# First batch by query tiles with its channel mix among the weight loads, score pieces in pairs, and x by head pair

## The chip, the core and the metric

One core of a Trainium2 chip runs the whole program. The metric is device time in microseconds (us) of one execution. The kernel before takes 312.73 us (median of 3 runs, 312.42 to 312.89). Five engines work side by side, each in the order in which its own instructions were written: TensorE (PE, with its weight loads as PEld), VectorE (DVE), ScalarE (ACT), GpSimd (POOL) and SyncE (SP), which here issues all DMAs. They wait for each other by semaphores.

## The reference

Blockwise causal attention, followed by an RWKV channel mix with a shift by one token.

```
q, k, v: (8 batches, 8 heads, 576 tokens, 64)     block = 64
scores = q @ k.T / 8, kept where query block >= key block
attn = softmax(scores);   x = (attn @ v) as (batch, token, head * 64 = 512)
x_prev = x shifted by one token, zeros at a batch's start
xk = mu_k * x + (1 - mu_k) * x_prev;   xr = the same with mu_r
k = relu(xk @ w_k)                (512 -> 1024)
out = sigmoid(xr @ w_r) * ((k * k) @ w_v)
```

All inputs and outputs are float32.

## The kernel before

**Attention, by batch.** The 576 tokens of a batch are four tiles of 128 and a tail of 64. For each of 4 head pairs `add_qk` loads q and k (four DMAs of 128 KB), POOL casts them to bf16, PE transposes them (8 matmuls of 128 columns), DVE copies the result out of PSUM into `t_qkt`; a tail transposes the last 64 tokens of all heads. `add_score` computes the scores of a head pair in three pieces (512, 64 + 448 and 320 + 192 query columns), with keys as the stationary operand. The two heads of a pair lie on partitions 0 to 63 and 64 to 127, so their two matmuls run side by side. ACT takes the exponential of each piece (128 x 1024) into `t_e`; POOL sets masked blocks to zero. `add_last` does the last 64 x 64 blocks of all heads. `add_av` multiplies by v (15 matmuls of 65 columns a head; the 65th column is the sum of the exponentials), and DVE normalises into x (`t_x`). When all heads of the batch are done, `add_xt` transposes x by token tiles, and ACT copies it to `t_xt`.

**Channel mix, by chunk.** The 8 x 576 tokens are 9 chunks of 512. `add_mix` makes xk and xr: a difference of neighbours (two on DVE, two on POOL), a repair of the column at a batch's start on both engines, and 8 multiply-adds on DVE. `add_pk` is xk @ w_k in 8 groups of 4 matmuls of 512 columns, relu on ACT, square on DVE; `add_pr` is xr @ w_r with tanh on ACT (4 groups of 4); `add_pv` is the second product (4 groups of 8), and DVE combines and SP stores it.

**What sets the order.** All of these are tasks of a planner (`Plan`). Each has an engine, an estimated length, a rank, the tasks that it depends on, and buffers of rings that it takes (`RINGS`: 10 load buffers, 2 score buffers `s`, 2 of `m` for transposes and the product with v, 2 of `mm` for the channel mix; these three are PSUM). The planner runs a list schedule over these estimates and writes the instructions out in that order, so ranks and estimated lengths decide what stands behind what on each engine. Batch b has ranks around 13 b, and batch 0 stands 40 lower (`step`, L174); chunk c's matmuls begin at `step(c + 1, 6) + LAG` (L693). The loads of w_k are ranked after batch 0's, and those of w_r and w_v after batch 1's (L656 to L674).

Of the kernel before, what the change touches and what calls it, by code (L numbers as in the profile page):

```python
# [9 lines left out]
FP = mybir.dt.float32  # L10
# [3 lines left out]
ALU = mybir.AluOpType  # L14


class Plan:
# [24 lines left out]
    def order(self):  # L42
# [8 lines left out]
        while waiting:  # L51
            moved, nxt = False, []
            for e, q in todo.items():
# [3 lines left out]
                for n, t in enumerate(q):  # L57
# [46 lines left out]
def kernel(  # L104
# [12 lines left out]
    nc = tc.nc  # L117
# [16 lines left out]
             "x": 1, "r": 4, "xt": 2, "d": 1, "xk": 2, "xr": 2, "kr": 3,  # L134
# [25 lines left out]
    MUR = consts.tile([P, CCn], FP)  # L160

# [35 lines left out]
    def add_qk(b, pr, rank):  # L197
        nb = plan.buf("nb")
        tiles["nbbuf", b, pr] = nb
        for n, src in enumerate((q, k)):  # L200
# [8 lines left out]
            def fn(n=n, key=key):  # L209
# [6 lines left out]
                "POOL", 0.62, rank, fn,  # L216
                [t] + ([cast["qk", b, pr, 0]] if n else []),
                takes=[nb] if n == 0 else [],
                uses=[ld] + ([nb] if n else []))

    def add_tail(b, rank):
# [12 lines left out]
        cast["tb", b] = on("POOL", 0.62, rank, fn, [t], takes=[tb], uses=[tl])  # L234

    def add_v(b, rank, halves):
        bufs = [plan.buf("vl") for _ in range(5)]
        for half in range(halves):
            nh = H // halves
            hs = slice(half * nh, half * nh + nh)  # L240
            for sc in range(5):
                n = P if sc < 4 else D
                t = load(("vl", b, sc),
                         (lambda: new("vl", [P, H, D], FP)) if half == 0 else None,
                         lambda d, n=n, sc=sc, hs=hs: [(
                             d[0:n, hs], v[b, hs, sc * P:sc * P + n].rearrange(
                                 "h p d -> p h d"))],
                         rank[half], 0.0011 * n * nh,
                         takes=[bufs[sc]] if half == 0 else [],
                         uses=[] if half == 0 else [bufs[sc]])  # L250

                def fn(n=n, sc=sc, hs=hs):
                    nc.gpsimd.tensor_copy(VOs[b % 2][0:n, sc, hs, 0:D],
                                          tiles["vl", b, sc][0:n, hs])
                first = half == 0 and sc == 0
                cast["v", b, half, sc] = on(
                    "POOL", 0.12 + 0.001 * nh * D, rank[half], fn,
                    [t] + ([] if first else [cast["v", b, 0, 0]]),
                    takes=[vo_buf[b]] if first else [],
                    uses=[bufs[sc]] + ([] if first else [vo_buf[b]]))  # L260

    def add_w(name, n, rank):
        src = {"k": moe_w_k, "r": moe_w_r, "v": moe_w_v}[name]
        src = src.rearrange("(cc p) (n j) -> n cc p j", p=P, j=C)
        for i in range(n):
# [4 lines left out]
                     rank, 0.7, takes=[ld])  # L270

            def fn(i=i, cc=cc, half=half):
# [9 lines left out]
                "DVE" if name == "k" else "ACT", 0.4 if name == "k" else 0.56,  # L282
# [5 lines left out]
    def add_qkt(b, pr, rank):  # L288
# [27 lines left out]
        def ev():  # L316
# [4 lines left out]
            if pr < HP:  # L321
# [22 lines left out]
    def add_score(b, pr, i, rank):  # L344
        s = plan.buf("s")
        if i == 0:
            tiles["ebuf", b, pr] = plan.buf("e")
        ebuf, qbuf = tiles["ebuf", b, pr], tiles["qktbuf", b]

        def fn():  # L350
            if i == 0:
                tiles["e", b, pr] = new("e", [P, 2, 3, 512], F16)
            PS = tiles["ps", b, pr, i] = new("s", [P, 2, 512], FP)
            qkt = tiles["qkt", b]
            for (col, kc, q0, n) in PIECES[i]:
# [24 lines left out]

    def add_last(b, rank):
# [30 lines left out]
    def add_av(b, h, rank, halves):  # L412
# [3 lines left out]
        if h == 0:  # L416
            tiles["xbuf", b] = plan.buf("x")
# [313 lines left out]
```

## Time and profile before

| | |
|---|---|
| median of 3 runs | 312.73 us |
| the profiled execution | 312.19 us |
| its span, first to last instruction | 310.4 us |
| PE busy | 274.2 us, 88% of the span |
| DVE, ACT, POOL busy | 225.2, 186.0, 124.8 us |
| first matmul starts, last one ends | 4.9 us, 305.5 us |
| read from HBM, written | 33.56 MB, 9.44 MB |

A matmul's busy time includes the time that it spends in the pipeline beside the next one, so busy shares of PE say only that it had something in flight; its throughput is read from the starts of consecutive groups. The granted clock (PEclk) has two levels here, 1.00 (2.4 GHz) and 0.50 (1.2 GHz).

### The profile page before, as it was taken

Reading aid. Unit: us, or ns where it says so; the run is one execution under the profiler, and the core shown is the slowest. Engines: PE = TensorE matmul, PEld = TensorE weight load, DVE = VectorE, ACT = ScalarE, POOL = GpSimd, SP = SyncE. Lnnn points to the kernel's source line nnn. Section 1 sums busy time; section 2 is a strip of 40 time slices with the busy share of each in tenths; the row PEclk is TensorE's granted clock in tenths of the full one; section 3 lists DMA queues with packets and bytes.
Section 4 is the critical chain, followed back from the end, with each engine's and each line's share of the span. In section 5 each row is a group of like instructions: output and inputs, shape, how many; then the busy total and the mean of one; then the engine's idle time right before and its main releaser. Section 6 shows DMA issues by size and latency. Waiting matters only on the chain. (4 is left out here: it accounts for less than half of the span.)

```text
span 310.4 us, 6718 instructions
## 1 busy us (share of the span) xinstructions
PE 274.2 (88%) x2512; PEld 150.5 (48%) x2512; DVE 225.2 (73%) x407; ACT 186.0 (60%) x269; POOL 124.8 (40%) x279
## 2 busy tenths in 40 slices
PE   1883889899569979999999999989999999889993
PEld 0452545366345634564456545644555456334441
DVE  3265589464989599849796978697869677998541
ACT  1761559968447737785678567855795584252530
POOL 3660772467957682473276224610033004120000
PEclk9998759999899999999999999999999999999998
DMA  6989999999999988999963610012001200201102
GB/s 155 220 193 246 205 235 363 212 220 199 206 230 240 229 213 221 205 208 231 241 140 81 143 68 2 2 64 74 1 2 55 83 2 34 99 7 68 68 34 102
DMA packets 122769, 43.44 MB, mean 140 GB/s; under 512 B 115568, under 2 KB 115568, under 8 KB 122736
## 3 DMA queue, kind: packets, MB, share of 16 engines
q1 hardware_dynamic: 122736, 43.01, 58.0%
q8 instruction: 19, 0.31, 0.5%
q14 instruction: 14, 0.11, 0.1%
HBM read 33.56 MB, written 9.44 MB: 139 GB/s over the span
## 5 line engine op out<-in xcount | busy, mean ns | idle before, releaser
L368 ACT ACTIVATE t_e<-t_s 128x1024 f16<-128x1024 f32 x96 | 95.7, 1026 | 48.6 <-PE t_s L358 48.3
L573 PE MATMUL t_mm<-t_xk,WK 128*128 128x512 f16 x288 | 70.2, 383 | 4.1 <-DVE t_xk L549 2.2
L626 PE MATMUL t_mm<-WV,t_k 128*128 128x512 f16 x288 | 67.3, 379 | 5.1 <-DVE t_o L636 4.8
L590 DVE TENSOR_TENSOR t_k<-t_kr 128x512 f16<-128x512 f32 x72 | 53.5, 756 | 11.8 <-ACT t_kr L584 11.6
L584 ACT ACTIVATE t_kr<-t_mm 128x512 f32<-128x512 f32 x72 | 43.1, 599 | 27.0 <-PE t_mm L573 24.8
L212 POOL CAST t_nb<-t_ld 128x512 bf16<-128x512 f32 x64 | 43.0, 680 | 36.8 <-DMA t_ld<-in_q_dram 19.6
L376 POOL MEMSET t_e<- 64x128 f16 x128 | 23.6, 199 | 82.0 <-ACT t_e L368 77.8
L626 PEld LDWEIGHTS <-t_k 128*128 128x128 f16 x288 | 27.2, 98 | 36.2 <-issue 8.3
L426 PEld LDWEIGHTS <-t_e 128*128 128x128 f16 x896 | 34.7, 99 | 17.4 <-issue 5.8
L573 PEld LDWEIGHTS <-WK 128*128 128x128 f16 x288 | 25.7, 98 | 34.8 <-issue 10.3
L358 PE MATMUL t_s<-t_qkt 64*128 64x512 bf16 (+4 forms) x320 | 37.6, 313 | 5.4 <-ACT t_e L368 3.2
L426 PE MATMUL t_m<-VO,t_e 128*128 128x65 f16 x896 | 38.9, 196 | 3.8 <-DVE t_x L444 2.9
L636 DVE SCALAR_TENSOR_TENSOR t_o<-t_t,t_mm 128x512 f32<-128x512 f32 x36 | 24.6, 684 | 23.3 <-PE t_mm L626 16.8
L603 PE MATMUL t_mm<-WR,t_xr 128*128 128x512 f16 x144 | 36.2, 380 | 0.0
L613 ACT ACTIVATE t_t<-t_mm 128x512 f32<-128x512 f32 x36 | 21.5, 597 | 21.9 <-PE t_mm L603 21.8
L444 DVE TENSOR_TENSOR t_x<-t_m,t_r 128x320 f32<-128x320 f32 x64 | 31.5, 492 | 2.2
L492 ACT COPY t_xt<-t_m 128x512 f32<-128x512 f32 (+1 forms) x44 | 20.8, 521 | 17.6 <-PE t_m L482 17.6
L523 POOL TENSOR_TENSOR t_d<-t_xt 128x512 f32<-128x512 f32 x18 | 23.8, 1336 | 18.0 <-issue 9.8
L523 DVE TENSOR_TENSOR t_d<-t_xt 128x512 f32<-128x512 f32 x18 | 19.6, 1119 | 15.4 <-ACT t_xt L492 15.3
L549 DVE SCALAR_TENSOR_TENSOR t_xk<-t_d,MUK,t_xt 128x512 f16<-128x512 f32 x36 | 30.1, 874 | 0.3
L303 PE MATMUL t_m<-identb,t_nb 128*128 128x128 bf16 x256 | 23.4, 240 | 6.9 <-POOL t_nb L212 6.6
L322 DVE COPY t_qkt<-t_m 128x1024 bf16<-128x1024 bf16 x32 | 21.6, 677 | 9.9 <-PE t_m L303 9.6
(39 smaller groups left out, 218.9 us busy)
## 6 DMA issues: line engine op xcount, KB each, us to landing
out_dram<-t_o SPq DMA_DIRECT2D x36, 256.0 KB, 2.0
t_ld<-in_q_dram SPq DMA_DIRECT2D x64, 128.0 KB, 3.4
t_ld<-in_k_dram SPq DMA_DIRECT2D x64, 128.0 KB, 3.4
t_vl<-in_v_dram SPq DMA_DIRECT2D x28, 256.0 KB, 4.7
t_ld<-in_moe_w_k_dram SPq DMA_DIRECT2D x8, 256.0 KB, 5.6
t_ld<-in_moe_w_v_dram SPq DMA_DIRECT2D x8, 256.0 KB, 5.8
t_vl<-in_v_dram SPq DMA_DIRECT2D x15, 128.0 KB, 3.8
t_tl<-in_q_dram SPq DMA_DIRECT2D x8, 128.0 KB, 4.2
```

The source lines that it names most:

```text
L212: nc.gpsimd.tensor_copy(tiles["nb", b, pr][:, n], tiles[key][:, :].rearrange("p t h d -> p t (h d)"))
L358: nc.tensor.matmul(PS[:, h, col:col + n], qkt[rows, pr, 1, kc * P:kc * P + P], qkt[rows, pr, 0, q0:q0 + n], start=True, stop=True)
L368: nc.scalar.activation(tiles["e", b, pr][:, :, i, :], tiles["ps", b, pr, i], AF.Exp, scale=ISQ)
L426: nc.tensor.matmul(PA[:, mt * D1:(mt + 1) * D1], stationary(b, h, kc, mt), VOs[b % 2][:, kc, h, 0:D1], start=(kc == 0), stop=(kc == mt))
L444: nc.vector.tensor_tensor(tiles["x", b][:, :, h * D:(h + 1) * D], view[:, :, 0:D], Rc[:, :].unsqueeze(2).to_broadcast([P, 5, D]), ALU.mult)
L523: (nc.vector if eng == "DVE" else nc.gpsimd).tensor_tensor(tiles["d", c][:, cc], x[:, cc, 1:CH + 1], x[:, cc, 0:CH], ALU.subtract)
L549: nc.vector.scalar_tensor_tensor(tiles[name, c][:, cc], tiles["d", c][:, cc], (MUK, MUR)[n][:, cc:cc + 1], tiles["xt", c][:, cc, 1:CH + 1] ...
L573: nc.tensor.matmul(ps, WK[:, cc, jc * P:(jc + 1) * P], tiles["xk", c][:, cc], start=(cc == 0), stop=(cc == CCn - 1))
L584: nc.scalar.activation(tiles["kr", c, jc], tiles["pk", c, jc], AF.Relu)
L590: nc.vector.tensor_tensor(tiles["k2", c][:, jc], KR, KR, ALU.mult)
L603: nc.tensor.matmul(ps, tiles["xr", c][:, cc, jt * P:(jt + 1) * P], WR[:, cc], start=(cc == 0), stop=(cc == CCn - 1))
L626: nc.tensor.matmul(ps, tiles["k2", c][:, jc, jt * P:(jt + 1) * P], WV[:, jc], start=(jc == 0), stop=(jc == JCn - 1))
```

## The change

Six things change.

1. Batch 0 is loaded, transposed, scored and multiplied by query tiles of 128 tokens rather than by head pairs (`add_qk_tile`, `add_first`, `add_first_av`, `add_first_xt`), and chunk 0's channel mix is done per tile (`add_first_mix`, `add_first_pk` with 128-column matmuls), with the loads of all weights among its own.
2. Scores of later batches are planned two pieces at a time (`add_scores`).
3. x is kept by head pair (`x` ring 4), transposed as soon as a head pair is done, and mixed per head pair (`add_xt`, `add_mix`, `d` ring 3 of a quarter's size).
4. The repair at a batch's start is two small products on POOL behind the multiply-adds; it leaves DVE.
5. Ranks stand in a table, estimated lengths are raised (0.62 to 0.68, 0.73 to 0.82 and the like), chunk c's matmuls begin at `step(c) + 25`.
6. The planner may take two buffers of one ring for one task.

```diff
+RANK = {
+ 'loads': ['q0', 'wk0', 'v0', 'mu', 'wk7', 'wk1', 'wv2', 'wk2', 'wk3',
...
-             "x": 1, "r": 4, "xt": 2, "d": 1, "xk": 2, "xr": 2, "kr": 3,
+             "x": 4, "r": 4, "xt": 2, "d": 3, "xk": 2, "xr": 2, "kr": 3,
...
+    def add_scores(b, items, rank):
...
+        for it in items:
+            s = plan.buf("s")
+            bufs.append(s)
+            takes.append(s)
...
+        def fn():
             qkt = tiles["qkt", b]
-            for (col, kc, q0, n) in PIECES[i]:
-                for h in range(2):
-                    rows = slice(h * D, h * D + D)
+            for it in items:
+                PS = tiles["ps", b, it] = new("s", [P, 2, 512], FP)
...
+                for pr, col, kc, q0, n in mms:
+                    for h in range(2):
+                        rows = slice(h * D, h * D + D)
+                        nc.tensor.matmul(
+                            PS[:, h, col:col + n],
+                            qkt[rows, pr, 1, kc * P:kc * P + P],
+                            qkt[rows, pr, 0, q0:q0 + n], start=True, stop=True)
...
+    FIRST = {
+        0: [(0, 0, [0], P, [0, 1, 2, 3])],
+        1: [(0, 512, [0, 1], P, [0, 1]), (0, 1024, [0, 1], P, [2, 3])],
+        2: [(1, 384 * pr, [0, 1, 2], P, [pr]) for pr in range(4)],
+        3: [(2 + pr // 2, 768 * (pr % 2) + 384 * i, [2 * i, 2 * i + 1], 192,
+             [pr]) for pr in range(4) for i in range(2)],
+    }
...
+    def add_xt(b, pr, rank):
...
+            for i in range(4):
+                src = (tiles["x", b, pr][:, i] if pr < HP
+                       else tiles["x", b, i][:, 4])
...
+    def add_mix(c, cc, rank):
...
+                    def fix(n=n, at=at, name=name):
+                        nc.gpsimd.tensor_tensor(
+                            tiles[name, c][:, :, at:at + 1],
+                            tiles["xt", c][:, :, at + 1:at + 2],
+                            (MUK, MUR)[n][:, :].unsqueeze(2), ALU.mult)
...
+    def add_first_pk(mt, g, rank):
...
+            for j in range(4):
+                jc = 4 * g + j
+                for cc in range(CCn):
+                    nc.tensor.matmul(
+                        ps[:, j * P:(j + 1) * P],
+                        WK[:, cc, jc * P:(jc + 1) * P],
+                        tiles["xk", 0][:, cc, ts], start=(cc == 0),
+                        stop=(cc == CCn - 1))
...
+        for n in range(0, len(order), 2):
+            add_scores(b, order[n:n + 2], r + n)
...
-        first = step(c + 1, 6) + LAG
+    for c in range(1, NCH):
+        first = step(c, R["moe"])
```

The order on SP at the program's start, before (`t_ld` are load buffers of q, k and weights, `t_tl` the tails, `t_vl` v; x4 means four in a row):

```order
L185 DMA t_vl<-in_v_dram 64x4x64
L659 DMA MUK<-in_moe_mu_k_dram 128x4x1
L660 DMA MUR<-in_moe_mu_r_dram 128x4x1
L185 DMA t_ld<-in_moe_w_k_dram 128x512 x8
L185 DMA t_ld<-in_q_dram 128x4x64 x2
L185 DMA t_ld<-in_k_dram 128x4x64 x2
...
L185 DMA t_vl<-in_v_dram 128x8x64 x4
L185 DMA t_vl<-in_v_dram 64x8x64
L185 DMA t_ld<-in_moe_w_r_dram 128x512 x4
L185 DMA t_ld<-in_moe_w_v_dram 128x512 x8
```

And now, on SP, from the program's first DMA to the tails of batch 0:

```order
L218 DMA t_ld<-in_q_dram 128x8x64
L218 DMA t_ld<-in_k_dram 128x8x64
L218 DMA t_ld<-in_moe_w_k_dram 128x512
L218 DMA t_vl<-in_v_dram 128x8x64
...
L218 DMA t_ld<-in_moe_w_k_dram 128x512 x2
L218 DMA t_ld<-in_moe_w_v_dram 128x512
L218 DMA t_ld<-in_moe_w_k_dram 128x512 x5
...
L218 DMA t_ld<-in_moe_w_r_dram 128x512 x3
...
L218 DMA t_ld<-in_moe_w_v_dram 128x512 x6
L218 DMA t_tl<-in_q_dram 64x8x64
L218 DMA t_tl<-in_k_dram 64x8x64
```

All weights now stand ahead of batch 0's tail and of all of batch 1's loads; before, w_r and w_v came behind batch 1's.

The order on PE in front of chunk 1's first channel-mix matmul, before (with tile numbers; `t_mm_1564` is that matmul's output, `VO0` with `t_e` the product with v of batch 2):

```order
L426 MATMUL t_m_1506<-VO0_130,t_e_1367 128x65
...
L390 MATMUL t_s_1526<-t_qkt_1456 128x64
...
L303 MATMUL t_m_1542<-identb_120,t_nb_1385 128x128
...
L573 MATMUL t_mm_1564<-t_xk_1324,WK_134 128x512
```

And now, on PE, the same place:

```order
L592 MATMUL t_m_1525<-VO0_130,t_e_1371 128x65
...
L592 MATMUL t_m_1546<-VO0_130,t_e_1371 128x65
...
L348 MATMUL t_m_1576<-identb_120,t_nb_1543 128x128
...
L427 MATMUL t_s_1585<-t_qkt_1139 128x320
...
L427 MATMUL t_s_1590<-t_qkt_1139 128x512
...
L662 MATMUL t_m_1600<-identf_125,t_x_1524 128x128 x4
L800 MATMUL t_mm_1611<-t_xk_1185,WK_134 128x512
```

Now chunk 1's matmuls begin behind the second head of batch 2 (t_m_1546), whose product needs all of batch 2's v; before they began behind its fifth.

The order on PE in a later batch, before (`t_s` are score buffers):

```order
L358 LDWEIGHTS t_qkt_2626
L358 MATMUL t_s_3166<-t_qkt_2626 128x512
L573 LDWEIGHTS WK_134
L573 MATMUL t_mm_3173<-t_xk_2946,WK_134 128x512
...
L303 MATMUL t_m_3181<-identb_120,t_tb_2264 128x128
...
L358 MATMUL t_s_3188<-t_qkt_2626 128x64
...
L358 MATMUL t_s_3188<-t_qkt_2626 128x448
L303 LDWEIGHTS t_nb_2643
```

And now, on PE, the same kind of place:

```order
L427 LDWEIGHTS t_qkt_2576
L427 MATMUL t_s_2960<-t_qkt_2576 128x512
...
L427 MATMUL t_s_2964<-t_qkt_2576 128x64
...
L427 MATMUL t_s_2964<-t_qkt_2576 128x448
L800 LDWEIGHTS WK_134
L800 MATMUL t_mm_2971<-t_xk_2193,WK_134 128x512
```

Two score buffers are now filled in one visit, where a channel-mix group and four transposes stood between them. Over the whole program PE changes from other work to scores 82 times before and 59 times now.

## Rows read from the trace of the kernel before

**Rows 1.** Stretches: PE, PEld, DVE, ACT, POOL busy (count), PEclk, DMA share, GB/s

```profile
0.00:18.30 18.30, 10.58 (x107) 6.50 (x107) 6.10 (x17) 7.66 (x8) 10.28 (x31) 1.00 0.93 192
18.30:28.50 10.20, 5.24 (x103) 3.48 (x99) 5.68 (x16) 5.70 (x6) 3.02 (x12) 1.00 0.82 224
28.50:35.30 6.80, 5.39 (x27) 4.38 (x28) 2.85 (x10) 2.72 (x5) 2.51 (x4) 0.50 1.07 209
...
38.80:45.60 6.80, 5.66 (x38) 2.93 (x38) 6.18 (x8) 4.08 (x6) 5.29 (x13) 0.50 1.02 222
45.60:60.00 14.40, 13.49 (x126) 6.94 (x125) 11.09 (x22) 13.21 (x24) 4.44 (x9) 1.00 1.03 300
60.00:79.60 19.60, 18.22 (x219) 11.09 (x219) 11.54 (x21) 15.41 (x22) 13.92 (x31) 1.00 1.06 204
79.60:91.80 12.20, 7.14 (x99) 5.10 (x99) 10.29 (x20) 5.17 (x6) 9.69 (x23) 0.86 1.08 233
...
200.00:260.00 60.00, 58.38 (x561) 31.68 (x559) 47.28 (x88) 39.06 (x57) 11.23 (x36) 1.00 0.10 36
```

**Rows 2.** Timeline of PE, chunk 1's first matmuls: start, length in us

```profile
88.74 0.81 PE L573 MATMUL t_mm<-t_xk,WK 128*128 128x512 f16 x3
91.80 1.46 PE L573 MATMUL t_mm<-t_xk,WK 128*128 128x512 f16 x6 [2.25 <-DVE t_xk L549]
```

**Rows 3.** Waits from 60 to 92 us: total, times, longest

```profile
PE t_m L426 <- DVE t_x L444: 2.6, 1, 2.6
...
PE t_mm L573 <- DVE t_xk L549: 2.2, 1, 2.2
```

**Rows 4.** Timeline of PE in a stretch without waits, 184 to 190 us

```profile
184.50 0.61 PE L303 MATMUL t_m<-identb,t_nb 128*128 128x128 bf16 x8
185.05 0.39 PE L358 MATMUL t_s<-t_qkt 64*128 64x512 bf16 x2
185.37 1.04 PE L573 MATMUL t_mm<-t_xk,WK 128*128 128x512 f16 x4
186.24 0.39 PE L303 MATMUL t_m<-identb,t_tb 128*128 128x128 bf16 x4
...
188.63 0.60 PE L426 MATMUL t_m<-VO,t_e 128*128 128x65 f16 x14
189.06 0.19 PE L426 MATMUL t_m<-VO,EL 128*128 128x65 f16 x1
189.09 0.61 PE L303 MATMUL t_m<-identb,t_nb 128*128 128x128 bf16 x8
189.54 1.89 PE L573 MATMUL t_mm<-t_xk,WK 128*128 128x512 f16 x8
```

**Rows 5.** Timeline of PE, transposes of x at 201 us

```profile
201.69 1.04 PE L482 MATMUL t_m<-identf,t_x 128*128 128x128 f32 x8
202.56 1.03 PE L603 MATMUL t_mm<-WR,t_xr 128*128 128x512 f16 x4
```

**Rows 6.** Page, GB/s moved in each of 40 slices of 7.76 us

```profile
GB/s 155 220 193 246 205 235 363 212 220 199 206 230 240 229 213 221 205 208 231 241 140 81 143 68 2 2 64 74 1 2 55 83 2 34 99 7 68 68 34 102
```

**Rows 7.** Page, costly groups: busy us, mean ns of one, idle before

```profile
L368 ACT ACTIVATE t_e<-t_s 128x1024 f16<-128x1024 f32 x96 | 95.7, 1026 | 48.6 <-PE t_s L358 48.3
...
L584 ACT ACTIVATE t_kr<-t_mm 128x512 f32<-128x512 f32 x72 | 43.1, 599 | 27.0 <-PE t_mm L573 24.8
```

**Rows 8.** Groups by line: last blocks' exponential, multiply-adds, the small edge copy

```profile
L549 DVE SCALAR_TENSOR_TENSOR t_xk<-t_d,MUK,t_xt 128x512 f16<-128x512 f32 x36 | 30.1, 874 | 0.3
...
L399 ACT ACTIVATE EL<-t_s 64x512 f16<-64x512 f32 x8 | 4.7, 589 | 0.6 <-PE t_s L390 0.2
...
L508 DVE COPY t_xt<-t_xt 128x4 f32<-128x4 f32 x8 | 1.7, 210 | 0.0
```

**Rows 9.** Timeline of ACT, copies of x of two sizes

```profile
31.30 0.59 ACT L492 COPY t_xt<-t_m 128x512 f32<-128x512 f32 x1 [7.08 <-PE t_m L482]
...
34.89 0.37 ACT L492 COPY t_xt<-t_m 128x256 f32<-128x256 f32 x1 [0.35 <-PE t_m L482]
```

**Rows 10.** Waits over the whole span: total, times, longest

```profile
PE t_s L358 <- ACT t_e L368: 3.2, 5, 1.0
```

More of the change, by code (lines that the diff above doesn't have):

```diff
@@ L233, in fn @@
                 tiles["tb", b], tiles["tl", b][:, :].rearrange("p h d -> p (h d)"))
[L234 to L260, printed above, removed]
@@ L262, in add_w, with add_v, fn @@
-    def add_w(name, n, rank):
+        cast["tb", b] = on("POOL", 0.68, rank, fn, [t], takes=[tb], uses=[tl])
+    def add_v(b, ranks):
+        for sc in range(5):
+            n = P if sc < 4 else D
+            vl = plan.buf("vl")
+            t = load(("vl", b, sc), lambda: new("vl", [P, H, D], FP),
+                     lambda d, n=n, sc=sc: [(
+                         d[0:n], v[b, :, sc * P:sc * P + n].rearrange(
+                             "h p d -> p h d"))],
+                     ranks[sc], 0.0088 * n, takes=[vl])
+            def fn(n=n, sc=sc):
+                nc.gpsimd.tensor_copy(VOs[b % 2][0:n, sc, :, 0:D],
+                                      tiles["vl", b, sc][0:n])
+            cast["v", b, sc] = on(
+                "POOL", 0.68, ranks[sc], fn, [t],
+                takes=[] if sc else [vo_buf[b]],
+                uses=[vl] + ([vo_buf[b]] if sc else []))
@@ new lines, in fn, with add_edge, edge @@
+                    px[:, cc * P:(cc + 1) * P], tiles["x", 0, mt][:, cc],
+                    identf, is_transpose=True, start=(cc == 0),
+                    stop=(cc == CCn - 1))
+        t = on("PE", 0.46, rank, fn, [evac["x0", mt, g] for g in range(2)],
+               takes=[m], uses=[tiles["xbuf", 0, mt]])
+        n, off = (P, 0) if mt < 4 else (D, D)
+        to_xt(key, 0, mt * P, n, off, None, [t], rank, [m])
+    mixed = {}
+    def add_edge(c, rank):
+        def edge():
+            nc.vector.tensor_copy(xt_tile(c)[:, :, 0:1],
+                                  tiles["xt", c - 1][:, :, CH:CH + 1])
+        take = not xt_parts[c]
+        t = on("DVE", 0.21, rank, edge, list(xt_parts[c - 1]),
+               takes=[xtbuf[c]] if take else [],
+               uses=[xtbuf[c - 1]] + ([] if take else [xtbuf[c]]))
+        xt_parts[c].append(t)
+        for x in range(CCn):
+            xt_of[c].setdefault(x, []).append(t)
@@ L585, in relu @@
                                  AF.Relu)
-        t = on("ACT", 0.56, SOON, relu, [t], takes=[kr], uses=[m])
+        t = on("ACT", 0.6, SOON, relu, [t], takes=[kr], uses=[m])
         def sq():
@@ new lines, in mu1 @@
+        nc.vector.tensor_scalar_add(MUR1, MUR, -1.0)
+    R = RANK
+    at = {x: -99 + i for i, x in enumerate(R["loads"])}
+    for mt in range(4):
+        add_qk_tile(mt, at[f"q{mt}"])
+    add_tail(0, at["t"])
+    add_v(0, [at[f"v{sc}"] for sc in range(5)])
+    t = on("SP", 0.6, at["mu"], mus, [])
+    mu_ready.append(on("DVE", 0.3, at["mu"], mu1, [t]))
+    for name, n in (("k", 8), ("r", 4), ("v", 8)):
+        add_w(name, n, [at[f"w{name}{i}"] for i in range(n)], R["cast " + name])
+    for n, mt in enumerate((0, 1, 2, 3, HP)):
+        add_qkt(0, mt, R["qkt0"][n])
```

544 lines of the change are left out of this document (356 added, 188 removed), and 17 rows, old and new, of the table RANK.

## The prediction

> **What bounds the kernel now.** I read the stretches first [rows 1]. From 91.8 us on PE has something in flight nearly always (58.38 of 60 us between 200 and 260), no other engine does (DVE 47.28), and the DMA share is 0.10 there: the second part is bound by PE. The first part is not. Up to 18.3 us PE works 10.58 us, then 5.24 of 10.20, and from 79.6 to 91.8 only 7.14 of 12.20, while the DMA share is 0.82 to 1.08. The granted clock is 0.50 (1.2 GHz) from 28.5 to 35.3 and from 38.8 to 45.6, each time behind a stretch with idle time. The first part is bound by the arrival of data and by chains through PE, ACT and DVE that have too little work of PE beside them.
>
> A busy share does not say how much PE got done, so I price its work by the starts of neighbouring groups where nothing waits [rows 4, 5]. Eight transposes take 189.54 - 189.09 = 0.45 us, 0.056 each. Four matmuls of 512 columns take 186.24 - 185.37 = 0.87 us, 0.2165 each. Fifteen matmuls of 65 columns take 189.09 - 188.63 = 0.46 us, 0.030 each. Eight f32 transposes of x take 202.56 - 201.69 = 0.87 us, 0.109 each. A visit to the scores costs extra: eight transposes ahead of scores take 185.05 - 184.50 = 0.55 us, 0.10 more than ahead of a channel-mix group, and the two score matmuls of 512 columns, which run side by side, take 185.37 - 185.05 = 0.32 us where 512 columns take 0.2165. So going in and coming out cost 0.20 us together.
>
> With these prices the program before has 960 products with v (28.8 us), 288 transposes (16.1), 160 of x (17.4), 720 channel-mix matmuls (155.9), scores of 51,200 columns per head of a pair (100 x 0.2165 = 21.7) and 82 visits (16.4): 256.3 us of work. PE is at it from 4.9 to 305.5 us, so some 44 us are lost to waits and the slow clock. Most of that goes before chunk 1's channel mix gets going at 91.80 us [rows 2]: the work in front of it is 315 products (9.5), 136 transposes (7.6), 40 of x (4.4), 80 matmuls of chunk 0 (17.3), scores (8.2) and 24 visits (4.8), together 51.8 us, and 0.6 more for the three matmuls at 88.74. So 39 us are lost up to 91.8 us, and 9 to 10 in the 213.7 us after it.
>
> **Part by part: PE's work.** Pairs of pieces cut the visits from 82 to 59: 23 x 0.20 = 4.6 us less. Chunk 0's first product is now 128 matmuls of 128 columns with a weight load each instead of 32 of 512. The nearest row is the transposes, which have the same shape and also a weight load each: 128 x 0.056 = 7.2 against 32 x 0.2165 = 6.9 us, 0.3 more. Below that it can't go, since the columns are the same; 0.05 more for each would be 6 us, but nothing in the rows points there. Batch 0's scores have the same number of columns. New total: 256.3 - 4.6 + 0.3 = 252.0 us.
>
> A page of the Trainium skill speaks against those small matmuls: "TensorE: Matmul & The Clock Gate", section "Back-to-back issue gap", gives some 81 ns for each of a stream of weight load and matmul pairs of 128 columns. By it they would cost 10.4 us, and the kernel up to 3.2 us more than I forecast, if PE were the last to be ready there. The trace does not agree: pairs of just this shape go at 56 ns [rows 4], and I keep to that.
>
> **Part by part: where chunk 1 begins.** In the new order of PE there stand in front of chunk 1's first matmul 270 products (8.1), 128 transposes (7.2), 44 of x (4.8), 48 matmuls of 512 columns (10.4), the 128 small ones (7.2), scores of 16,640 columns (7.0) and 21 visits (4.2): 48.9 us. Behind it are 252.0 - 48.9 = 203.1 us, before 256.3 - 52.4 = 203.9. So what follows is 0.8 us shorter, and where the waits in it stay as they are, the span is T + (310.4 - 91.8) - 0.8 = T + 217.8 us, where T is the time at which chunk 1's matmuls begin. The whole prediction is this T.
>
> T is bounded by DMA. The first matmul of chunk 1 stands behind the second head of batch 2, which needs all of batch 2's v. Of q, k and v a batch has 3.54 MB, the weights 5.24 MB: 3 x 3.54 + 5.24, less the last head pair of batch 2 (0.52, loaded later), plus four stores of chunk 0 (1.05) is 16.4 MB. The slices of 7.76 us add up to 16.4 MB at about 72 us [rows 6]; their first ones hold idle time of the DMAs (shares of 0.93 and 0.82 [rows 1]) that the new order, which asks for all weights at once, can fill in part. So 67 to 72 us for the last byte, and 1.5 us for cast and products: T is not under 68.
>
> T is also bounded by ACT. Batch 0's tile 3 waits for the tail, now loaded behind all the weights and most of batch 0: 8.4 MB. At the slices' own rates that is 41 us; with weights at the 363 GB/s of the slice that held mostly weights and the rest at 205 it would be 5.24 / 0.363 + 3.15 / 0.205 = 30 us after a start of 2.5. So tile 3's exponentials begin between 34 and 43 us. From there ACT has, in its order up to the products of batch 2's first head pair, 15 exponentials of 1.026 (15.4), 8 of three quarters of that size (0.8 each by size, 6.4), three for the last blocks (1.8), four relu and two tanh of 0.6 (3.6) [rows 7, 8], and copies of x: two of 0.59, two of 0.37 [rows 9], and four pairs that I take at 0.75, since each splits 512 columns in two (4.9 in all): 32 us. ACT was busy 92% of the densest stretch and 79% of the one after it [rows 1]. From 34 us at full load T would be 67, from 43 us at 75% it would be 87. I take the middle, 38 us and 85%, with 1.5 us for the last zeros and products: T = 78. That is the step on which most depends.
>
> What else stands in this part. Chunk 0's 32 small multiply-adds on DVE (128 columns) replace eight of 512: between the edge copy's 0.21 us and half of 0.874 each [rows 8], 7 to 14 us in place of 7. DVE has by my count some 60 us of work up to T, so up to 15 us more can hide in its gaps; if it did not, T would stand at the upper end. The repair at a batch's start leaves DVE for POOL, which adds about 0.3 us ahead of a chunk whose mix is ready long before it is needed: nothing. The edge copy stays. More but smaller copies of x cost ACT 0.7 us a batch; it was idle a third of the time from 200 to 260 us, so nothing. The stores of chunk 0 stand on SP in front of batch 1's and 2's later loads and could hold them up while PE is late; that is in the 72 us.
>
> Mixing by head pair also removes what held PE between 79.6 and 91.8 us: 2.6 us for DVE to normalise while it was in a block of multiply-adds, and 2.2 us for the last of the mix [rows 3]. Next to be late there are ACT's exponentials, which the bound above holds.
>
> **Sum.** Span 78 + 217.8 = 295.8 us. The profiled execution took 312.19 us with a span of 310.4, so 1.8 more outside it: 297.6 us. Its time is 0.5 us under the median of the runs shown, so I predict 297.5 us.
>
> **Rivals.**
> 1. The early start does not come off: T stays near 91.8, since DMA and ACT give out the same work at the same rate, and only the visits are saved. 91.8 + 217.8 + 1.8 = 311.4 us. For it speaks that DMA was full from 28.5 us on; against it that chunk 0's 17 us of channel mix, which stood behind all of batch 0 and in the middle of batch 1, can now run while the weights land.
> 2. Pairs make PE wait. With two score buffers, a pair's second piece can't start before the exponential of the previous pair's second piece is done, and PE takes its work in order. There are 42 full pairs. If each costs PE half an exponential (0.51 us), that is 21.5 us: 297.6 + 21.5 = 319 us, slower. From (312.7 - 297.6) / 42 = 0.36 us a pair it is slower than before. Against it: before, PE waited for ACT ahead of scores 5 times in all, 3.2 us [rows 10], and ACT is busy 39 of 60 us in the part that would suffer.
> 3. It goes better: T at the DMA bound of 69 us, and the waits after it halve from 10 to 5 us, as the planner's lengths are now nearer to the measured ones. 69 + 217.8 - 5 + 1.8 = 284 us.
>
> **Chances and range.** The forecast (T from 68 to 88) 0.77, rival 1 0.10, rival 2 0.06, rival 3 0.07. T from 68 to 88 gives 287.6 to 307.6 us; half of rival 3 lies near that, and nearly all of rival 1 above it. I set 286 to 309 us. A measurement of this kernel tells 0.2% (0.6 us) from no change. Of rival 1 I count half as faster and half as the same: faster 0.77 + 0.07 + 0.05 = 0.89, same 0.05, slower 0.06.
>
> **What would show it.** Chunk 1's first channel-mix matmul starts near 78 us and nothing of 2 us or more holds it up behind that; chunk 0's small matmuls follow each other at 0.056 us at the full clock; a visit with two pieces costs 0.20 us above its columns, and there are 59; PE waits little for ACT ahead of scores. It is wrong if T is above 88, if the clock is at 0.50 for more than the 17 us that it was before 92 us, or if the stretch from T to the end takes more than 222 us, which would be rival 2.

## The result and the profile after

The changed kernel takes 302.0 us (median of 4 runs, 300.1 to 303.9); the kernel before took 312.6 us beside it. The ratio is 0.967, with an interval of 0.960 to 0.974. In a later series it took 303.5 us (6 runs, 300.2 to 304.2; ratio 0.970, 0.965 to 0.974). The forecast was 297.5 us, with a range of 286 to 309: the side and the range are right, the time is 4.5 us too low, 6.0 in the later series. Slow executions are left out of the ratios: two of some 671 us (one of the kernel before, one of that kernel with new lengths) and the profiled one of fewer bytes of w_v (302.9 us), so that the T given for that version isn't a fast run's.

The page of the changed kernel, profiled in its longest execution of the first four (303.93 us, span 302.1), has these rows. Each digit is the busy share of a 40th of the span in tenths.

```profile
PE 265.2 (88%) x2648; PEld 154.0 (51%) x2648; DVE 228.2 (76%) x433; ACT 187.0 (62%) x296; POOL 127.1 (42%) x274
...
PE   2276499787769999999999999999999999999995
...
PEclk9999999999979999999999999999999999999999
DMA  8999999899899999999993811001101110211112
GB/s 164 310 252 261 215 205 226 193 215 238 190 209 215 204 192 256 227 211 213 232 244 68 173 55 73 2 0 72 69 2 37 71 38 0 103 39 69 69 37 104
```

PE's row has its 9s from the thirteenth slice on, DMA is full up to the 21st, and the recorded clock falls in one slice, at 83 to 91 us. The stretches that answer to [rows 1] (columns as there):

```profile
60.00:79.60 19.60, 14.68 (x222) 10.08 (x221) 14.02 (x31) 13.68 (x20) 13.80 (x28) 1.00 1.02 213
79.60:91.80 12.20, 9.20 (x106) 6.18 (x103) 9.34 (x18) 6.52 (x11) 9.69 (x21) 0.86 1.08 217
200.00:260.00 60.00, 59.59 (x545) 32.68 (x543) 48.71 (x90) 39.33 (x65) 14.25 (x40) 1.00 0.11 41
```

PE was in flight for 58.38 of the last stretch's 60 us, now for 59.59. The stretch just ahead of 91.8 us, whose waits were to go by the forecast, is still there, with PE idle for 3.0 of its 12.2 us. Its rows on PE:

```profile
84.47 0.19 PE L592 MATMUL t_m<-VO,EL 128*128 128x65 f16 x1
87.08 1.01 PE L348 MATMUL t_m<-identb,t_nb 128*128 128x128 bf16 x8 [2.42 <-DVE t_r L609]
88.03 1.04 PE L427 MATMUL t_s<-t_qkt 64*128 64x320 bf16 x6
88.99 1.11 PE L662 MATMUL t_m<-identf,t_x 128*128 128x128 f32 x4
89.90 2.18 PE L800 MATMUL t_mm<-t_xk,WK 128*128 128x512 f16 x8
```

T, the start of chunk 1's first 512-column matmul, is 89.90 us: 1.9 us earlier than in [rows 2], not 13.8. Ahead of it stand transposes of `t_nb`, q and k of batch 3. PE waits 2.42 us in front of them, for DVE by its row; what for is read below (fewer bytes ahead of T).

To compare kernels I apply the prediction's prices to PE's order: what is priced is work, what is left of the time is lost (waits, slow clock, and some 4.5 us before the first matmul). From the traces by one list (products with v at 0.029 us; the end is the start of the last matmul):

| kernel, profiled execution | T | work, lost ahead of T | work, lost behind T | all work, all lost | median of its runs |
|---|---|---|---|---|---|
| before | 91.8 | 52.1, 39.7 | 202.4, 10.9 | 254.6, 50.5 | 312.6 |
| after | 89.9 | 48.7, 41.2 | 201.8, 6.2 | 250.5, 47.4 | 302.0 |
| after, later series | 87.6 | 48.7, 38.9 | 201.8, 8.2 | 250.5, 47.1 | 303.5 |
| pieces one at a time | 92.3 | 52.5, 39.8 | 202.4, 10.0 | 254.9, 49.8 | 310.7 |
| fewer bytes of w_v | 85.7 | 48.7, 37.0 | 201.8, 9.5 | 250.5, 46.5 | 300.0 |
| mix waits for all of x | 94.1 | 50.2, 43.9 | 200.3, 7.1 | 250.5, 51.0 | 308.1 |
| before, with pairs | 92.9 | 48.6, 44.2 | 200.5, 15.6 | 249.2, 59.8 | 315.8 |
| load length 1.6 | 80.4 | 46.5, 33.9 | 204.0, 8.3 | 250.5, 42.2 | 298.4 |
| 1.6 and fewer bytes | 80.2 | 46.5, 33.8 | 204.0, 8.3 | 250.5, 42.1 | 297.7 |
| load length 2.0 | 83.8 | 45.0, 38.8 | 205.1, 17.9 | 250.1, 56.7 | 310.5 |
| old lengths | 84.0 | 48.2, 35.8 | 202.3, 8.3 | 250.5, 44.1 | 303.3 |
| mixes at one rank | 88.2 | 49.1, 39.2 | 201.4, 5.6 | 250.5, 44.7 | 300.7 |
| 1.6 and one rank | 83.0 | 46.4, 36.6 | 204.1, 8.1 | 250.5, 44.7 | 300.1 |
| before, new lengths | 90.6 | 51.2, 39.4 | 202.8, 9.8 | 254.0, 49.1 | 309.1 |

The profiled executions of before and after differ by 8.3 us: 4.1 us less work, 3.1 us less lost, and 1.1 us in what follows the last matmul's start. Each row is one execution, and T differs between executions of one kernel (89.9 and 87.6), so differences of 2 us between rows say little.

### The profile page after: what moved, and what is told of

Same layout as the page of the kernel before. It is cut to its first block, busy times and chain, and to the rows that moved or that the text cites. A ratio compares the mean times of both kernels' runs of the same rounds, so it can differ in the third digit from the quotient of the medians.

```text
span 302.1 us, 7058 instructions
## 1 busy us (share of the span) xinstructions
PE 265.2 (88%) x2648; PEld 154.0 (51%) x2648; DVE 228.2 (76%) x433; ACT 187.0 (62%) x296; POOL 127.1 (42%) x274
## 4 chain that ended last, share of the span: by engine, by line
PE 58%; DMA 15%; DVE 10%; SPq 6%; POOL 5%; ACT 3%; issue 2%; POOLq 0%; DVEq 0%
PE t_mm L888 16%; PE t_mm L800 16%; PE t_mm L865 7%; DMA t_ld<-in_k_dram 6%; SPq L218 6%; PE t_m L592 6%; PE t_s L427 5%; PE t_m L662 4%; PE t_m L348 3%; DMA t_ld<-in_q_dram 2%; DMA t_tl<-in_k_dram 2%; DMA t_ld<-in_moe_w_k_dram 2%; POOL t_nb L245 2%; DVE t_xk L728 2%; DVE t_xr L728 2%
## 5 line engine op out<-in xcount | busy, mean ns | idle before, releaser
L448 ACT ACTIVATE t_e<-t_s 128x1024 f16<-128x1024 f32 x84 | 84.2, 1030 | 18.7 <-PE t_s L427 18.0
L800 PE MATMUL t_mm<-t_xk,WK 128*128 128x512 f16 x256 | 61.3, 381 | 0.2 <-DVE t_o L899 0.2
L815 DVE TENSOR_TENSOR t_k<-t_kr 128x512 f16<-128x512 f32 x64 | 47.4, 745 | 8.1 <-ACT t_kr L809 7.5
L300 POOL CAST VO<-t_vl 128x512 f16<-128x512 f32 (+1 forms) x40 | 30.4, 775 | 12.6 <-DMA t_vl<-in_v_dram 9.7
L592 PEld LDWEIGHTS <-t_e 128*128 128x128 f16 x784 | 28.9, 97 | 12.6 <-POOL t_e L456 4.1
L592 PE MATMUL t_m<-VO,t_e 128*128 128x65 f16 x784 | 32.1, 193 | 3.5 <-POOL t_e L456 3.0
L641 ACT COPY t_xt<-t_m 128x256 f32<-128x256 f32 (+7 forms) x68 | 23.5, 391 | 15.8 <-PE t_m L662 14.2
L427 PE MATMUL t_s<-t_qkt 64*128 64x64 bf16 (+4 forms) x344 | 28.3, 278 | 0.0
L728 DVE SCALAR_TENSOR_TENSOR t_xr<-t_d,MUR,t_xt 128x512 f16<-128x512 f32 x32 | 26.8, 841 | 0.2 <-PE t_mm L865 0.2
L716 POOL TENSOR_TENSOR t_d<-t_xt 128x512 f32<-128x512 f32 x16 | 18.5, 1159 | 16.7 <-ACT t_xt L641 10.6
```

The lines of the kernel that those rows point to most:

```text
L300: nc.gpsimd.tensor_copy(VOs[b % 2][0:n, sc, :, 0:D], tiles["vl", b, sc][0:n])
L427: nc.tensor.matmul(PS[:, h, col:col + n], qkt[rows, pr, 1, kc * P:kc * P + P], qkt[rows, pr, 0, q0:q0 + n], start=True, stop=True)
L448: nc.scalar.activation(tiles["e", b, pr][:, :, i, :], tiles["ps", b, it], AF.Exp, scale=ISQ)
L592: nc.tensor.matmul(PA[:, mt * D1:(mt + 1) * D1], stationary(b, h, kc, mt), VOs[b % 2][:, kc, h, 0:D1], start=(kc == 0), stop=(kc == mt))
L728: nc.vector.scalar_tensor_tensor(tiles[name, c][:, cc], tiles["d", c, cc], (MUK1, MUR1)[n][:, cc:cc + 1], tiles["xt", c][:, cc, 1:CH + 1], ...
L800: nc.tensor.matmul(ps, WK[:, cc, jc * P:(jc + 1) * P], tiles["xk", c][:, cc], start=(cc == 0), stop=(cc == CCn - 1))
```

## Experiments: what the gain is made of

Differences from the changed kernel are from its first median, 302.0 us. From its later one, 303.5 us, a slower version loses 1.5 us less and a faster one gains 1.5 us more.

**Pieces one at a time.** In the changed kernel:

```
-        for n in range(0, len(order), 2):
-            add_scores(b, order[n:n + 2], r + n)
+        for n in range(len(order)):
+            add_scores(b, order[n:n + 1], r + n)
```

> The changed kernel with score pieces planned one at a time again. PE's visits to the scores go from 59 back to 82. Theory 1 (a visit costs PE 0.20 us wherever PE is the bound): 3 to 5 us more than the changed kernel's 302.0 us, so 305 to 307. Rival 1 (pairs cost PE as much in waits for the exponentials as they save): 301 to 303. If the early part, which is not bound by PE, holds many of the saved visits, 303 to 304.

It took 310.7 us (ratio to before 0.995, 0.992 to 0.997), 8.7 us more than the changed kernel and above all that was expected. Of the 6.8 us between the two profiled ends 4.4 are work (82 visits for 59 at 0.19) and 2.4 more losses. What PE waited for behind 90 us (us in total, times, longest):

```profile
PE t_m L662 <- DVE t_x L610: 2.4, 3, 1.5
PE t_mm L800 <- POOL t_xk L743: 1.7, 1, 1.7
PE t_mm L800 <- ACT t_kr L809: 1.4, 2, 0.7
```

The visits' price can be read in the traces: behind 95 us, in visits without idle time, it is 0.20 us above the columns (median of 36 in the changed kernel, most of them with two pieces, and of 51 here). The rest comes with the other order that the planner makes; that single pieces leave less of PE's work between dependent steps would explain the 1.4 us for ACT's relu between groups of the channel mix, but no run takes this by itself.

**Mix of a pair only when all of x is there.**

```
-                 list(xt_of[c][cc]), takes=[d], uses=[xtbuf[c]])
+                 [p for x in range(CCn) for p in xt_of[c][x]], takes=[d], uses=[xtbuf[c]])
```

> The changed kernel, but no head pair of a chunk is mixed before x of all four is there, so the mix comes in a block as before the change. Theory 3 (waits of PE behind chunk 1's start fell from about 10 to 5 us because DVE's mix comes in pieces and no longer holds up the evacuation of PSUM): 3 to 6 us more, 305 to 308, with PE's waits for DVE's combination (t_o) back at several us. Rival 3 (they fell because the planner's lengths are nearer the measured ones): 301 to 303.

308.1 us (ratio 0.987, 0.984 to 0.990), 6 us more. On PE:

```profile
87.74 0.61 PE L427 MATMUL t_s<-t_qkt 64*128 64x64 bf16 x8
94.06 2.29 PE L800 MATMUL t_mm<-t_xk,WK 128*128 128x512 f16 x5 [5.72 <-POOL t_xk L743]
```

and on POOL, which makes the repaired column last:

```profile
93.36 0.65 POOL L743 TENSOR_TENSOR t_xk<-t_xt,MUK 128x4 f16<-128x4 f32 x1 [0.62 <-DVE t_xk L728]
```

DVE is at multiply-adds up to that row, and chunk 1 waits 5.72 us for the last. Mixing by head pair takes this one wait away. Ahead of T 2.7 to 5.0 us more are lost than in the changed kernel's two traces; behind it the loss lies between theirs. PE's waits for the combination ahead of a second product come to 0.8 us and not to the several that theory 3 expected: the time is theory 3's, its reason isn't.

**Pairs alone, in the kernel before.** `add_score` and `add_last` are replaced by the new `add_scores` (at 0.98 for an exponential; the last blocks' goes from 0.55 to 0.6, and a pair counts 0.64 on PE for twice 0.44), and the planner may take two buffers of a ring.

```
+        for n in range(0, len(order), 2):
+            add_scores(b, order[n:n + 2], r + n)
```

> The kernel before with score pieces in pairs and nothing else changed; visits go from 82 to 54. Theory 1: 28 x 0.20 = 5.6 us less work, of which the part ahead of 92 us may be lost in waits: 307 to 310 us against 312.6. Rival 1 (pairs make PE wait for ACT): 312 to 318, with PE's waits for the exponentials ahead of scores well over 3 us.

315.8 us (ratio 1.010, 1.007 to 1.013): slower. The work is 5.4 us less (54 visits), the losses 9.3 us more. Ahead of T:

```profile
82.57 0.40 PE L380 MATMUL t_s<-t_qkt 64*128 64x64 bf16 x4 [0.90 <-ACT t_e L401]
83.48 0.40 PE L380 MATMUL t_s<-t_qkt 64*128 64x320 bf16 x4 [0.52 <-ACT t_e L401]
89.74 0.93 PE L435 MATMUL t_m<-VO,t_e 128*128 128x65 f16 x14 [5.86 <-POOL VO L256]
```

PE's 5.86 us are for the cast of v, which stands on POOL behind casts of q and k and two differences of the mix (1.37 and 1.47 us):

```profile
82.30 1.37 POOL L532 TENSOR_TENSOR t_d<-t_xt 128x512 f32<-128x512 f32 x1
...
85.67 1.47 POOL L532 TENSOR_TENSOR t_d<-t_xt 128x512 f32<-128x512 f32 x1
...
88.54 1.17 POOL L256 CAST VO<-t_vl 128x512 f16<-128x512 f32 x2
```

ACT's exponentials cost little here too: ahead of T PE waits 2.2 us for them in all, of which the two waits above are 1.4. So pairs gain or lose by the order that they are put in. Without them the changed kernel takes 8.7 us more, and with them the old one takes 3 us more. Neither number is what pairs are worth elsewhere.

**Estimated lengths.** In the changed kernel the old ones, and in the kernel before the new ones, for the work that both have (casts, exponentials, relu, square, combination, mix). One of each:

```
-            "DVE", 0.82, SOON, sq,
+            "DVE", 0.73, SOON, sq,
```

> The changed kernel with the planner's estimated lengths of before for the work that both have (casts 0.62 for 0.68, exponentials 0.98 for 1.03, relu and tanh 0.56 for 0.6, square 0.73 for 0.82, combination 0.69 for 0.78, differences 0.68 and 1.07 for 0.8 and 1.3, multiply-adds 0.76 for 0.78, edge copy 0.3 for 0.21). Theory 1 (the 4.8 us that PE waited for DVE's combination of the second product's result after T in the kernel before went away because the lengths are now nearer to those measured): these waits come back, 3 to 5 us of them, and the time is 305 to 307 us. Theory 2 (they went away because the mix is spread over the head pairs): at most 1 us of them comes back, and the time stays at 301 to 304 us.

> The kernel before with the new estimated lengths for the work that both have, and nothing else. Theory 1 (lengths alone remove the waits for the combination, 4.8 us): 307 to 309 us. Theory 2 (the structure of the mix does): 311 to 314 us, with 3 us or more of these waits left.

Old lengths in the changed kernel: 303.3 us, with runs from 300.5 to 307.7 (302.4 without the last; ratio 0.971, 0.967 to 0.976), no difference that can be told. New lengths in the kernel before: 309.1 us (ratio 0.990, 0.987 to 0.993), 3 us faster. PE's waits for the combination ahead of a second product, after T, in the first,

```profile
PE t_mm L888 <- DVE t_o L899: 2.2, 3, 1.6
```

and in the second:

```profile
PE t_mm L626 <- DVE t_o L636: 2.3, 3, 1.1
```

In the kernel before they were 4.8 us, in the changed one 0 and 0.5 in its two traces. By one trace each, the lengths account for about half of what went, in either kernel, and neither theory holds alone. But in the run with pairs alone, which keeps the old lengths, these waits were already down to 0.2 us (1.6 with those ahead of the other channel-mix matmuls), and with single pieces in the changed kernel there are none. So they follow the order as a whole, and no single part can be said to remove them.

**Mixes at one rank.**

```
-            add_mix(b, pr, r + R["mix"] + 3 * pr)
+            add_mix(b, pr, r + R["mix"] + 3 * HP)
```

> The changed kernel with the four head pairs' mixes of a chunk at one rank, that of the last of them, instead of three apart. The difference of a pair may still start as soon as its x is there. Theory 1 (spreading the multiply-adds over the batch is what removed PE's 4.8 us of waits for DVE's combination): DVE works off a chunk's eight multiply-adds closer together, waits of PE for the combination come back by 2 to 5 us, and the time is 304 to 307 us. Theory 2 (the lengths removed them): the time stays at 301 to 304 us and waits for the combination under 1 us.

300.7 us (ratio 0.963, 0.960 to 0.967), no slower than the changed kernel, with 0.7 us of these waits. Spreading the ranks isn't what removed them, and what did stays open.

## Experiments: what sets T

**Fewer bytes ahead of T.** Only 64 of 512 columns of each load of w_v are read, 1.84 MB less:

```
-                     lambda d, cc=cc, half=half: [(d, src[half, cc])],
+                     (lambda d, cc=cc: [(d[:, 0:64], src[0, cc][:, 0:64])])
+                     if name == "v" else
```

> The changed kernel, loading 64 of the 512 columns of each block of w_v and spreading them over the block, so 1.84 MB less is read (the output then uses a wrong w_v). Theory 2 (chunk 1's matmuls begin at 89.9 us because two head pairs and the tail of batch 3 are transposed in front of them on PE, and their loads land last, the DMAs being full): loads behind w_v land 6 to 8 us earlier, chunk 1 begins at 83 to 85 us, the whole takes 5 to 7 us less, 295 to 297. Rival 2 (the chain of POOL's casts and zeros, DVE and ACT sets that start, with data there in time): chunk 1 begins within 2 us of 89.9 and the time is 300 to 303.

300.0 us (ratio 0.958, 0.955 to 0.961), 2 us less than the changed kernel in one series, 3.5 less than in the other. In its profiled execution (the longest of six) T is 85.70:

```profile
83.58 0.61 PE L353 MATMUL t_m<-identb,t_nb 128*128 128x128 bf16 x8 [2.41 <-DVE t_r L614]
...
85.70 2.61 PE L805 MATMUL t_mm<-t_xk,WK 128*128 128x512 f16 x6
```

T falls by 2 to 4 us, just short of theory 2; the time is rival 2's. The bytes alone would have given some 5 us: an estimate, 1.84 MB at the 363 GB/s of the slice that held mostly weights [rows 6], not at the 213 GB/s of stretches with q, k and v. The same wait of 2.4 us stands there as before. What holds it can be read on POOL and DVE of the changed kernel:

```profile
80.73 1.05 POOL L285 CAST t_tb<-t_tl 128x512 bf16<-128x512 f32 x1 [0.73 <-DMA t_tl<-in_k_dram]
...
82.11 1.01 POOL L245 CAST t_nb<-t_ld 128x512 bf16<-128x512 f32 x1
...
83.59 0.62 POOL L245 CAST t_nb<-t_ld 128x512 bf16<-128x512 f32 x1
84.16 1.05 POOL L716 TENSOR_TENSOR t_d<-t_xt 128x512 f32<-128x512 f32 x1
...
86.33 0.62 POOL L245 CAST t_nb<-t_ld 128x512 bf16<-128x512 f32 x1 [0.57 <-DMA t_ld<-in_k_dram]
```

```profile
85.24 1.06 DVE L728 SCALAR_TENSOR_TENSOR t_xk<-t_d,MUK,t_xt 128x512 f16<-128x512 f32 x1 [1.24 <-POOL t_d L716]
...
86.44 0.49 DVE L610 TENSOR_TENSOR t_x<-t_m,t_r 128x320 f32<-128x320 f32 x1
86.85 0.18 DVE L609 RECIPROCAL t_r<-t_m 128x5 f32<-128x5 f32 x1
```

A batch has eight casts of `t_nb`, q and k of four head pairs. Counted from the program's start, those at 82.11 and 83.59 are the 27th and 28th: batch 3's second head pair, whose transposes begin at 87.08. They end at 84.21, so PE doesn't wait for these bytes. The casts at 85.14 and 86.33 are the third pair's, which is transposed behind T; the expectation of the next run, which has the bytes for these transposes land at 86.3 us, misreads them. What PE waits for is DVE, as its row says: the products of two heads hold both buffers of the ring `m`, which the transposes need too, and DVE has normalised the first at 86.93. Ahead of that DVE has a multiply-add that waits 1.24 us for POOL's difference, and POOL, without a gap of 0.1 us since 80.73, makes that difference behind the tail's cast and two more casts of batch 3. Late bytes have 0.73 us in this, POOL's wait for the tail. The rest is the order: casts of batch 3 in front of the difference, and its transposes in front of T.

**Transposes of batch 3 behind T.** No instruction added or removed; the planner takes a load of q, k or a tail as 1.6 instead of 1.2 (three places like this):

```
-                     rank, 1.2, takes=[ld])
+                     rank, 1.6, takes=[ld])
```

> The changed kernel with one number of the planner altered: the length that it assumes for loads of q, k and tails, 1.2 to 1.6. No instruction is added or removed, but no transpose of batch 3 stands ahead of chunk 1's first 512-column matmul (T) any more: 108 transposes there instead of 128. Theory 1 (T came late, at 89.9 us, because the transposes of batch 3's first two loaded head pairs and its tail stand ahead of it and wait for bytes that landed at 86.3 us; batch 2's last v landed at 73.3): T falls to 78 to 82 us, and since chunk 1's matmuls then fill PE while batch 3's loads land, the time falls by most of that, to 293 to 297 us. Theory 2 (bytes arrive at their rate wherever T is put, and PE meets the same wait later): T falls as well, the waits after T rise from 6 us by as much, and the time is 300 to 303 us. If T stays at 88 us or later, something else than the loads of batch 3 holds it.

298.4 us (4 runs, 297.9 to 298.6; ratio 0.956, 0.952 to 0.959), the fastest version with the reference's whole computation. T:

```profile
79.94 0.59 PE L592 MATMUL t_m<-VO,t_e 128*128 128x65 f16 x14 [0.78 <-DVE t_x L610]
...
80.40 1.89 PE L800 MATMUL t_mm<-t_xk,WK 128*128 128x512 f16 x8
```

T is where theory 1 put it, so batch 3's work in front did hold it, though not by the arrival of its bytes alone, as read above. Of the 9.5 us against the first trace, 4.1 lie ahead of the last product that T needs (80.37 for 84.47) and 5.4 in what stood between that product and T. The time falls by 3.6 us (5.1 against the later series), between the theories: T is 7 to 9.5 us earlier, but 2.2 us of the work ahead of it went behind it, and 5.0 to 7.3 us less are lost ahead of T against 0.1 to 2.1 more behind it.

**Fewer bytes on top of it.** The two edits above together.

> The assumed load length of 1.6, and beside it only 64 of the 512 columns of each load of w_v are read and spread over the tile (1.84 MB less; the second product is then not the reference's). With the length alone chunk 1's first 512-column matmul (T) began at 80.4 us, 5.7 us behind the last v of batch 2 (74.7), in 296.8 us of span. Theory 1 (T is now set by the arrival of batch 2's v): T falls by 1.84 MB at about 213 GB/s, 8.6 us, or most of that, to 72 to 75 us, and the time by at least half of it, to 292 to 294.5 us. Theory 2 (T is now set by the work of ACT, DVE and POOL between the tail of batch 0 and the products of batch 2): T falls by at most 4 us, to 77 to 80, and the time stays at 296 to 299 us.

297.7 us (296.7 to 300.0; ratio 0.953, 0.949 to 0.958), and T:

```profile
80.25 1.89 PE L805 MATMUL t_mm<-t_xk,WK 128*128 128x512 f16 x8
```

1.84 MB less move T by 0.15 us, as theory 2 has it. But the run doesn't test theory 1, because the last v of batch 2 hardly came earlier (it landed at 74.1 us for 74.7). SP, which issues all loads, had to store a result of chunk 0 first and stood for DVE's combination 4.4 us in either run. Its wait from 30 to 90 us and its next row, first with the load length alone,

```profile
SPq L905 <- DVE t_o L899: 4.4, 1, 4.4
68.73 2.38 SPq L218 DMA_DIRECT2D t_vl<-in_v_dram  x3
```

and then with fewer bytes too:

```profile
68.59 2.02 SPq L218 DMA_DIRECT2D t_vl<-in_v_dram  x3
```

So what the bytes saved went into SP's waits: for this store, and ahead of chunk 0's first stores, where SP waits for DVE 3.6 us in place of 1.7. What a v that lands several us earlier would do to T isn't shown.

**A load length of 2.0.** The same edit with 2.0 in place of 1.6.

> The planner's assumed load length at 2.0 in place of 1.2 (57 visits to the scores, 59 at 1.2 and 1.6; 240 products with v, 100 transposes ahead of chunk 1, no batch 3 among them). Theory 1 (the farther the planner puts work behind the loads, the less PE is held up, and the saving of the 1.6 was not a chance of one order): T at 72 to 78 us, time 294 to 299 us. Theory 2 (what PE does earlier it waits for later, since bytes arrive at their rate): T as low, the waits after T above 9 us, and the time 299 to 303 us.

310.5 us (ratio 0.995, 0.992 to 0.998). Neither theory foresaw it: T is 83.8, and behind it 17.9 us are lost, most of them from 120 to 150 us. The stretch from 124 to 148 us, in the columns of [rows 1]:

```profile
124.00:148.00 24.00, 17.63 (x230) 11.90 (x230) 17.39 (x35) 16.74 (x26) 17.59 (x40) 0.93 0.33 83
```

The DMA share is 0.33 in a part where the changed kernel has it full. SP's own queue there, and the combination on DVE that it waits for:

```profile
125.46 1.01 SPq L218 DMA_DIRECT2D t_ld<-in_k_dram  x2
126.56 17.36 SPq L905 DMA_DIRECT2D out_dram<-t_o  x2
144.01 5.49 SPq L218 DMA_DIRECT2D t_vl<-in_v_dram  x5
```

```profile
142.86 0.68 DVE L899 SCALAR_TENSOR_TENSOR t_o<-t_t,t_mm 128x512 f32<-128x512 f32 x1
```

The product that it combines is on PE at

```profile
114.47 1.89 PE L888 MATMUL t_mm<-WV,t_k 128*128 128x512 f16 x8
```

so it could have been combined at 117. The planner put it on DVE behind a batch's attention; that it did so because it takes loads for slow is my reading, no run shows it. Until then it holds one of two buffers of the channel mix, a store waits for it on SP for 17.36 us, and five loads of v wait behind that store. PE does a channel-mix group at 117.28 and the next at 143.16; between them it has attention alone, in chains with nothing to fill them.

**Both that helped, and the changed kernel again.** Load length 1.6 with the mixes at one rank, and the changed kernel unaltered.

> Both changes of the planner's numbers that took something off: the assumed load length of 1.6 (298.4 us alone) and the mixes of a chunk at one rank (300.7 us alone). Theory 1 (they act at different places, the one ahead of T and the other on DVE's order after T, and add up): 296 to 298 us, with less than 7 us lost after T. Theory 2 (each was one of several orders within a microsecond or two of each other): 297.5 to 300.5 us.

> The changed kernel as it is, beside the three others, since its first four times spread by 3.8 us. If the spread was one of the chip: a median of 301 to 303 us, T at 88 to 91 us. If its first profiled execution (303.9 us, the longest of the four) was an odd one: T at 84 to 87 us and 1 to 3 us fewer of waits.

300.1 us (ratio 0.960, 0.957 to 0.964): they don't add up, and theory 2 holds. The changed kernel again took 303.5 us with T at 87.58, between the two expectations, and a median just above the first one's. The run to run spread is in it, and 2.3 us by which T was earlier are lost again behind it (38.9 and 8.2 for 41.2 and 6.2).

## Why the prediction was right in the number and wrong in its main step

- **PE's work: right.** 4.3 us less were forecast, 4.1 less are there by the same prices, and the traces bear out the two that are new: 0.20 us for a visit with two pieces, as read above, and for chunk 0's small matmuls the price of a transpose. In

```profile
59.52 0.61 PE L427 MATMUL t_s<-t_qkt 64*128 64x512 bf16 x6
60.06 0.60 PE L592 MATMUL t_m<-VO,t_e 128*128 128x65 f16 x14
...
60.98 1.06 PE L835 MATMUL t_mm<-t_xk,WK 128*128 128x128 f16 x16
61.87 1.03 PE L865 MATMUL t_mm<-WR,t_xr 128*128 128x512 f16 x4
```

  sixteen take 61.87 - 60.98 = 0.89 us, 0.056 each. The Trainium skill, "TensorE: Matmul & The Clock Gate", section "Back-to-back issue gap", has some 81 ns for such a pair; by an estimate from it the 128 would have taken 3.2 us more, and the trace does not show that.
- **T = 78 us: wrong, 89.9 and 87.6.** This is the step that failed, the first of the two above 88, the prediction's own sign of being wrong. (Its sum, 38 + 32 / 0.85 + 1.5, is 77.1 and not 78.) The bound by bytes held as far as it went: batch 2's v was put at 67 to 72 us and landed at 73.3, and its products came 10 us later. In the bound by ACT the start held: tile 3's exponentials begin at 39.15 us, 38 was taken. Two other terms were too small. From there to the first product of batch 2, and from it to T (columns of [rows 1]):

```profile
39.15:83.40 44.25, 36.30 (x516) 25.01 (x516) 33.56 (x74) 29.48 (x46) 29.54 (x58) 1.00 0.97 213
83.40:89.90 6.50, 4.06 (x51) 2.93 (x49) 4.62 (x10) 2.94 (x3) 5.10 (x11) 0.78 1.03 202
```

  ACT is busy for 29.48 of 44.25 us, 67% and not 85%: its 32 us of work took 6.6 us longer than forecast. And 1.5 us were taken from the products to T, where 6.50 passed (2.42 of them the wait, and with the clock at 0.78 of full speed on the mean): the 128 transposes that the prediction counts ahead of T include 20 of batch 3, and what these stand behind (POOL's casts, DVE, PSUM buffers) is in neither bound. The second term is shown by the run that puts them behind T: there T is 80.4, 3.4 us behind the first product of batch 2. That this is within 2.4 us of the forecast is in part luck, since ACT is at 70% there too (27.66 of 39.50 us). What keeps ACT waiting stays open.
- **"What follows stays as it is": wrong, and it made up for half of the error, by luck.** From T to the end of the span it is 302.1 - 89.9 = 212.2 us, not 217.8 (214.1 in the later series): 6.2 us are lost there and not 10.9. The forecast had these waits stay at about 10. PE's waits behind 90 us are now

```profile
PE t_m L662 <- DVE t_x L610: 1.7, 3, 1.1
...
PE t_mm L800 <- DVE t_o L899: 0.2, 1, 0.2
```

  where 4.8 us were for the combination alone. That is the second half of rival 3, which the prediction tied to an early T; it came without one. T and the losses behind it aren't independent either: the changed kernel's two traces differ by 2.3 us in T and by 0.3 in their sum.
- **Rival 2, waits of PE for ACT: not there.** Idle time ahead of the scores of later batches (the last number of a row):

```profile
L427 PE MATMUL t_s<-t_qkt 64*128 64x512 bf16 x56 | 11.1, 393 | 0.0
```

- **Rival 1, T at 91.8 and only the visits saved:** right on T within 2 to 4 us, wrong on the time, for the waits behind T.
- **Mixing by pair removes waits ahead of T: half right.** The wait for the last of the mix is gone (5.72 us in the run that mixes in a block, of which 2.7 to 5.0 us are net), but PE still waits 2.42 us for DVE to normalise behind a multiply-add, where it was 2.6. The clock in the profiled execution: 0.86 from 79.6 to 91.8 us is 12.2 x 0.14 / 0.5 = 3.4 us at 0.50, behind the wait shown above, where before three stretches made 17 us. In the later series' trace it falls in four slices (mean 0.975, 0.994 in the first), so this gain isn't firm.
- **The step from span to time** has a slip: the profiled execution was 0.5 us under the median, which makes 298.1 us and not 297.5.
- **Not tested by itself:** batch 0 by query tiles with its channel mix among the weight loads. No run has it alone, and what part of the 10 us is its own stays open.

## What to carry to other kernels

A bound on a point of PE needs all that the order puts in front of it: an in-order engine waits for what stands ahead, whether the point needs it or not, and casts and copies on other in-order engines pass a wait on. A store on the queue that issues the loads holds them until its result is there (4.4 us and 17.36 us here). In a kernel whose order comes from a planner, an edit is not worth a fixed amount: pairs were worth 8.7 us in one order and cost 3 in another, and one assumed length moved the time from 302 to 298 and to 310 us. Try such numbers on the chip, and read where PE runs out of independent work.

## What was not expected of the chip

A DMA share near 1 does not say that DMA binds. With the load length of 1.6 the stretch ahead of T reads

```profile
36.00:80.00 44.00, 37.76 (x523) 25.70 (x521) 34.78 (x75) 29.94 (x45) 27.57 (x59) 0.96 0.97 200
```

and with 1.84 MB less read

```profile
36.00:80.00 44.00, 37.61 (x527) 25.85 (x526) 33.83 (x75) 30.16 (x46) 26.49 (x56) 0.96 0.92 192
```

All loads of w_v are issued by 29 us, so the bytes that were saved lie ahead of this stretch, and what is read in it is nearly the same in the same time. Its loads hardly move up, and SP's waits go with that: from 30 to 90 us it waits 4.8 us for POOL's casts to free load buffers and 4.4 us for the store (with the load length alone). Only the run with fewer bytes and these waits told this; the rows of the kernel alone read as a bound by DMA.
